# A fused attention and mixture-of-experts kernel: routing steps left in line, three batches counted, other slots for query scaling and scatters

## The chip, the cores and the metric

The kernel runs on one core of a Trainium2 chip. The metric is device time in microseconds for one execution. Its engines are TensorE (PE, whose weight loads the profile lists as PEld), VectorE (DVE), ScalarE (ACT), GpSimd (POOL) and SyncE (SP). Each works through its own queue in order, and they wait for each other on semaphores. SP issues plain DMAs here; POOL issues the indirect ones, which gather or scatter rows by a list of row numbers.

## The reference

```python
B, H, S, D = 8, 8, 576, 64            # attention, causal in blocks of 64
scores = q @ k.T / sqrt(D);  scores[block_i < block_j] = -1e9
attn = exp(scores - max) / (sum + 1e-9)
x = (attn @ v), heads side by side     # 4608 rows of 512
logits = x @ w_gate + modality_bias[modality_id]      # 8 experts
e = argmax(logits);  g = softmax(logits)[e]
out = g * (relu(x @ w1[e]) @ w2[e])    # 512 -> 1024 -> 512, one expert per row
```

With the inputs drawn here three experts get rows: 2289, 2153 and 166 of the 4608. After three batches the counts are 828, 736 and 164, after four 1114, 1026 and 164.

## The kernel before

**Attention** runs over 32 pairs of heads, four pairs to a batch. The table `ORDER` is written out by hand: it is one slot, in which the queues of all engines get the steps of pair p = slot (first half) and of pair slot − 1 (second half). `S0` to `S3` are score products (L202), `M` row maxima on DVE (L209), `E` exponentials on ACT (L222), `T` transposes on PE (L229), `C` copies of them out of PSUM (L234, units 0, 1 and 5 on DVE, the others on ACT), `V` the products with v (L248), `O` copies of their results, `D` the inverse of the sums, `B` products with the identity and the gate weights (L268), `Z0` and `Z1` the scaled rows (L287). `L` loads q and k of a pair two slots ahead through SP, and `Q` scales q of the next pair on POOL (L184). The score products of slot n + 1 need `Q` of slot n. Six PSUM banks are shared: `S0` of the next slot writes the bank that `C0` has to empty first, `S1` that of `C1`.

**Routing.** After `Z1` of the last pair of a batch (slots 4, 8, ..., 32), SP stores the batch's rows in DRAM (L294, eight DMAs), and `routing` returns 19 small steps, mostly on DVE: logits, a product on PE (`total`), bias, maximum, exponential on ACT, one-hot, weight, stores, counts on PE, running positions. The names `q1` to `q6`, `qp` and `qv` in `ORDER` are the places where the next of them is taken off the list. Steps that are left when the next batch's `Z1` comes are emitted there at once. The last step leaves five scatters in `placing`; each is a small DVE add (L394) and a POOL scatter of 128 rows of 64 bytes into a list of row numbers by expert (L395), taken at `S0` and at `T0`.

**Choosing.** After EARLY = 4 batches `choose` appends 22 DVE steps (kind "c", L99) that pick the expert with most rows (a) and the next one (b). From slot 21 on `EARLY_STEPS` then does part of the experts' work inside the slots: `stage` loads weights of expert a through SP (L641, L644), `prep` splits them on POOL in eight instructions (L584, L585), `ids` loads row numbers, and `fetch` gathers 128 rows (L667) from the batches that were counted.

**The experts** work in segments of 256 rows: four `up` products of 24 matmuls (L706), each followed by a relu on ACT (L712) and its low part on DVE (L713); transposes of the next segment's rows (L688); two `down` products of 24 matmuls (L752), each with an output scatter on POOL (L755). Three lead segments use rows of the counted batches. `LAST` is slot 32: the end of the last pair woven with the `up` of the first lead segment. `run_all` then does its two `down`, the rest of the last batch's routing, all scatters that are left (`flush`), the loads of the lists for the other segments (L662), and loops over the segments; n = 1 is the second lead segment.

Of the kernel before, what the change touches and what calls it, by code (L numbers as in the profile page):

```python
# [25 lines left out]
PPB = H // 2  # L26
# [7 lines left out]
NROW = NE * REGION  # L34
COVER = SLOT * NSLOT
COVER_B = COVER - FEW
EARLY, NLEAD = 4, 3
LEAD = SLOT * NLEAD
BIG = float(1 << 20)
NWARM = 12  # L40
# [26 lines left out]
PARTS = (("idf", (128,)), ("ii", (128,)), ("iom8", (NE,)), ("iom40", (5, NE)), ("iov40", (5, NE)), ("inv5", (5,)), ("first5", (NE, 5)), ("base8", (NE,)), ("edges", (N // SLOT,)))  # L67

ORDER = (
# [3 lines left out]
)  # L73

EARLY_STEPS = {
    (21, "S0"): ("stage", "stage"), (21, "T0"): ("prep",),
    **{(slot, "T0"): ("stage", "prep") for slot in range(22, 29)},
    (28, "S0"): ("ids",), (29, "S0"): ("stage",),
    (30, "S0"): ("fetch",), (30, "T0"): ("fetch",),
    (31, "S0"): ("fetch",), (31, "T0"): ("fetch",),  # L80
}
LAST = (
    ("+turn0", 0), ("V", 1), ("O", 1), ("D", 1), ("+up0", 0), ("+relu", 0), ("B", 1), ("Z0", 1), ("Z1", 1), ("+place", 0), ("+up1", 0), ("+relu", 0), ("+up2", 0), ("+steps3", 0), ("+up3", 0), ("+place", 0),
    ("+relu", 0), ("+relu", 0), ("+turn1", 0), ("+steps2", 0),
)


# [20 lines left out]
def attention_moe(ctx, tc, qk, vr, bkw, mid, mb, w1, w2, cf, ci, ld, out):  # L108
# [382 lines left out]
    def run_slot(slot):  # L491
        nonlocal steps, ex
        if slot < NPAIR - 1:
            load_v(slot + 1)
        for name, stage in LAST if slot == NPAIR else ORDER:
            p = slot - stage
            if placing and slot < NPAIR and name in ("S0", "T0"):
                g, c = placing.pop(0)
                g(c)
            for what in EARLY_STEPS.get((slot, name), ()):  # L500
                if ex is None:
                    ex = Experts(ctx, tc, cst, scratch, btmp, con["edges"], xrows, idlist, idf, w1, w2, out, sel, run, base8, pick, dot, banks, (o0, banks[5]), placing, staging, extra, xrb)
                ex.early(what)
            if name[0:6] == "+steps":
                for f in steps[0 : int(name[6:])]:
                    f()
                steps = steps[int(name[6:]) :]
                continue
            if name[0] == "+":
                ex.early(name[1:])  # L510
                continue
            if name[0] == "q":
                kind = "" if name[1].isdigit() else name
                kinds = (kind,) if kind else ("", "c")
                quick = bool(steps) and getattr(steps[0], "kind", "") == "c"
                for _ in range(1 if kind else 3 if quick else 1 + (slot == PPB * EARLY + 1)):
                    if slot > 1 and steps and getattr(steps[0], "kind", "") in kinds:
                        steps.pop(0)()
                continue
            if not 0 <= p < NPAIR:  # L520
                continue
            emit(name, p)
            if name == "Z1" and p % PPB == PPB - 1:
                for f in steps:
                    f()
                steps = routing(p // PPB)
                if p // PPB == EARLY - 1:
                    choose(Later(dve, steps))

# [15 lines left out]


class Experts:
    def __init__(self, ctx, tc, cst, scratch, btmp, edges, xrows, idlist, idf, w1, w2, out, sel, run, base8, pick, dot, banks, ys, placing, staging, extra, xrb):
        self.__dict__.update(locals())
        self.nc = tc.nc  # L550
        self.turn, self.hturn = 0, 0
        self.er, self.w = {}, {}
        self.staged = []
        self.todo = [(k, name, c) for name in "abc" for k in range(2) for c in range(4)]
        self.sturn, self.sbank, self.tbank = 0, 0, 0
        flat = xrb[0].rearrange("p s q d -> p (s q d)")
        self.xg = [flat[:, 2 * XW * i : 2 * XW * i + 2 * XW].rearrange("p (a w) -> p a w", a=2) for i in range(2)]

        def cut(i, a, n=1024):
            return extra[:, i : i + n].rearrange("p (a f) -> p a f", a=a)  # L560

        self.w["a", 1] = [[cut(1024 * (4 * x + c), 2) for c in range(4)] for x in range(2)]
        self.xth, self.xtl = cut(1024 * 8, 4), cut(1024 * 9, 4)
        self.hidden = [[cut(1024 * (10 + i) + 512 * x, 2, 512) for x in range(2)] for i in range(4)]
        self.w["a", 0] = [cut(1024 * 14 + SHIFT + 4096 * x, 4, 4096) for x in range(2)]
        self.parts = []
# [9 lines left out]
    def early(self, what):  # L576
        if what == "stage":
            self.stage()
        elif what == "prep":
            st, k, name, c = self.staged[0]  # L580
            flat = [t.rearrange("p a f -> p (a f)") if len(t.shape) > 2 else t for t in (st, *self.target(k, name, c))]
            for i in range(4):
                s, h, l = (t[:, 256 * i : 256 * i + 256] for t in flat)
                self.nc.gpsimd.tensor_copy(h, s)  # L584
                self.nc.gpsimd.tensor_tensor(l, s, h, ALU.subtract)  # L585
            self.staged.pop(0)
        elif what == "ids":
            ids = self.load_ids(self.sel["ra"], 0, LEAD, "lead", ET.SP)
            self.plan = [(ids, 2 * t, "a", EARLY * S) for t in range(NLEAD)]
        elif what == "fetch":  # L590
            if not self.parts or not self.parts[-1].left:
                self.parts.append(self.fetch(*self.plan[len(self.parts)], early=True))
            s = self.parts[-1]
            row = self.cst.tile([128, 1], I32, name="row", bufs=4)
            self.nc.vector.tensor_copy(row, s.ids[:, s.t + s.left[0] : s.t + s.left[0] + 1])
            self.gather(s, row)
        elif what[0:4] == "turn":
            self.turn_rows(self.parts[int(what[4])], True)
        elif what[0:2] == "up":
            self.up_products(self.parts[0], int(what[2]))  # L600
        elif what == "place":
            if self.placing:
                g, c = self.placing.pop(0)
                g(c)
        elif what == "relu":
            self.up_relu(self.parts[0])
        elif what == "flush":
            self.flush()
# [164 lines left out]
        dve.tensor_copy(counti, count)  # L773
        return counti

    def run_all(self, steps):
        tc, ctx, nc, cst, sel, plan = self.tc, self.ctx, self.nc, self.cst, self.sel, self.plan
        dve = nc.vector
        self.wk = wk = ctx.enter_context(tc.tile_pool(name="wk", bufs=1, side="right", reuse_waits="tile"))
        self.w["b", 0] = [wk.tile([128, 4, DF], F32R, name=f"w0{x}b") for x in "hl"]  # L780
        wk.tile([128, SHIFT], F32R, name="pad0")
        w2 = [wk.tile([128, 2, DM], F32R, name=f"w1b{i}") for i in range(8)]
        wk.tile([128, SHIFT], F32R, name="pad1")
        self.w["b", 1] = [w2[0:4], w2[4:8]]
        s, nxt = self.parts
        later = self.fetch(*plan[2])
        self.down(s, 0)
        for f in steps[0:9]:
            f()
        self.down(s, 1)  # L790
        for f in steps[9:]:
            f()
        self.flush()
        s, nxt = nxt, later
        self.rem, left = (cst.tile([128, NE], F32, name=n) for n in ("rem", "left"))
        self.rowc, self.expc = (cst.tile([128, 1], I32, name=n) for n in ("rowc", "expc"))
        idsa = self.load_ids(sel["rr"], 0, COVER - LEAD, "a")
# [3 lines left out]
        idsc = self.load_ids(self.rowc, 0, SLOT, "c", most=NROW - SLOT)  # L801
        dve.tensor_tensor(left, self.run, sel["start"], ALU.subtract)
        self.more = self.trips(left)

        plan += [(idsa, 2 * t, "a") for t in range(NSLOT - NLEAD)]
        plan += [(idsb, 2 * t, "b") for t in range(NSLOT - 1)]
        plan += [(idsb, 2 * NSLOT - 2, "b", N, 1), (idsc, 0, "a")]
        for n in range(1, len(plan)):
            if s.parts == 1:
                self.up_few(s)  # L810
            else:
                for m2 in range(4):
                    self.up(s, m2)
                    if m2 == 1 and n < NSLOT:
                        self.convert(True)
            later = None
            if s.parts == 1:
                self.turn_few(s, 0)
# [1 line left out]
                self.hturn += 2  # L820
            if nxt is not None:
                self.turn_rows(nxt)
                if n + 2 < len(plan):
                    later = self.fetch(*plan[n + 2])
            if n >= NSLOT and self.staged:
                self.convert()
# [83 lines left out]
```

## Time and profile before

| | |
|---|---|
| three runs | 747.29, 748.56, 749.25 us; median 748.56 |
| the profiled execution | 747.08 us |
| its span, first to last instruction | 745.4 us |
| mean granted TensorE clock | 0.989 |
| PE busy | 724.3 us (97%) |
| DVE, ACT, POOL busy | 345.0, 332.2, 242.6 us |

Times in rows count from the first instruction of the profiled execution. A row of a timeline gives the start, the time until the last of the merged instructions ends, engine, line, operation, what it writes and reads, how many, and in brackets the idle time before it with what ended it. Attention fills about the first 300 us, the segments the rest.

### The profile page before, as it was taken

The numbers are of one execution on the slowest core, as the hardware profiler recorded it, in microseconds if no ns is written. First come the engines' busy times: TensorE is split into PE (matmuls) and PEld (weight loads), VectorE is DVE, ScalarE is ACT, GpSimd is POOL, SyncE is SP. The second block draws the span as 40 slices with busy tenths as digits, with TensorE's granted clock in tenths as the row PEclk, the third lists the DMA queues.
The fourth block names the chain that finished last, engine by engine and source line by source line (L and its number), as shares of the span: only waits on it lengthen the run. The fifth ranks groups of instructions, "written<-read, shape, count | busy, mean of one in ns | idle before, by whom it ended". The sixth has DMA issues, their size and how long they took to land. (4 is left out here: it accounts for less than half of the span.)

```text
span 745.4 us, 19432 instructions
## 1 busy us (share of the span) xinstructions
PE 724.3 (97%) x7800; PEld 633.5 (85%) x7800; DVE 345.0 (46%) x1036; ACT 332.2 (45%) x974; POOL 242.6 (33%) x326
## 2 busy tenths in 40 slices
PE   8999999999989999989999999999999999999995
PEld 5888888888778888978999889998899988999794
DVE  4888888988989987421221112211222122221220
ACT  5888877888767876212222222221222222221220
POOL 2223343433399964155223132232111221112101
PEclk9999999999999999998999999999999999999998
DMA  5476456464667672313221222213121221201000
GB/s 183 127 213 215 125 165 168 138 177 137 156 194 238 197 209 78 90 34 73 78 79 36 79 72 86 72 43 100 50 79 48 81 86 45 84 30 47 29 15 20
DMA packets 41916, 77.80 MB, mean 104 GB/s; under 512 B 12170, under 2 KB 24266, under 8 KB 41824
## 3 DMA queue, kind: packets, MB, share of 16 engines
q1 hardware_dynamic: 34336, 57.02, 26.3%
q0 software_dynamic: 7488, 19.52, 8.4%
q8 instruction: 62, 1.02, 0.6%
q14 instruction: 30, 0.25, 0.1%
HBM read 54.86 MB, written 22.25 MB: 103 GB/s over the span
## 5 line engine op out<-in xcount | busy, mean ns | idle before, releaser
L713 DVE SCALAR_TENSOR_TENSOR extra<-bank,extra 128x512 fp32r<-128x512 f32 x72 | 49.8, 692 | 313.8 <-ACT extra L712 313.8
L222 ACT ACTIVATE pm<-bank,nm 128x512 f32<-128x512 f32 (+3 forms) x320 | 155.6, 500 | 64.9 <-DVE nm L209 60.0
L209 DVE TENSOR_REDUCE nm<-bank 128x1 f32<-128x512 f32 (+3 forms) x320 | 121.0, 447 | 6.5 <-PE bank L202 6.0
L706 PE MATMUL bank<-extra 128*128 128x256 f32 x960 | 119.4, 285 | 2.7 <-issue 2.7
L706 PEld LDWEIGHTS bank<-extra 128*128 128x128 f32 x960 | 117.7, 192 | 4.4 <-issue 3.6
L712 ACT ACTIVATE extra<-bank 128x512 fp32r<-128x512 f32 x72 | 43.1, 598 | 158.6 <-PE bank L706 149.1
L229 PE MATMUL bank<-cf,pm 128*128 128x128 f32 (+1 forms) x736 | 90.7, 279 | 3.3 <-ACT pm L222 3.3
L706 PE MATMUL bank<-extra,w0hb 128*128 128x256 f32 x512 | 91.1, 280 | 0.0
L202 PE MATMUL bank<-raw,q 64*64 64x512 f32 (+7 forms) x1280 | 87.8, 407 | 2.5 <-POOL q L184 2.5
L229 PEld LDWEIGHTS bank<-cf,pm 128*128 128x128 f32 (+1 forms) x736 | 79.5, 140 | 11.3 <-ACT pm L222 7.0
L184 POOL TENSOR_SCALAR q<-raw 128x144 f32<-128x144 f32 x124 | 67.7, 573 | 59.4 <-PE bank L229 47.9
L202 PEld LDWEIGHTS bank<-raw,q 64*64 64x64 f32 x1280 | 54.9, 134 | 30.2 <-issue 21.1
L706 PEld LDWEIGHTS bank<-extra,w0hb 128*128 128x128 f32 x512 | 79.0, 188 | 0.7
L248 PE MATMUL b<-pt,v 64*64 64x64 f32 (+3 forms) x896 | 77.0, 267 | 0.9 <-issue 0.6
L248 PE MATMUL o<-pt,v 64*64 64x64 f32 (+3 forms) x896 | 72.5, 262 | 1.0 <-issue 1.0
L706 PE MATMUL bank<-extra,w0lb 128*128 128x256 f32 x256 | 71.8, 280 | 0.0
L755 POOL DMA_INDIRECT out<-scratch,ids_b x17 | 16.9, 994 | 161.8 <-ACT scratch L754 161.8
L234 DVE COPY pt<-bank 128x512 f32<-128x512 f32 (+1 forms) x96 | 59.2, 642 | 21.2 <-PE bank L229 15.6
L222 ACT ACTIVATION_READ_ACCUMULATOR pm<-bank,nm 128x1 f32 x320 | 65.2, 204 | 0.0
L395 POOL DMA_INDIRECT idlist<-idt,pi x40 | 40.3, 1008 | 73.8 <-DVE pi L394 67.6
L248 PEld LDWEIGHTS b<-pt,v 128*64 128x64 f32 (+1 forms) x896 | 54.7, 136 | 3.9 <-issue 1.0
L752 PE MATMUL o<-extra 128*128 128x512 f32 x240 | 57.2, 394 | 0.0
(149 smaller groups left out, 992.0 us busy)
## 6 DMA issues: line engine op xcount, KB each, us to landing
raw<-qk SPq DMA_DIRECT2D x31, 576.0 KB
v<-vr SPq DMA_DIRECT2D x32, 384.0 KB
staging<-w SPq DMA_DIRECT2D x24, 256.0 KB
staging<-w SPq DMA_DIRECT2D x12, 512.0 KB
xrows<-xr SPq DMA_DIRECT2D x16, 256.0 KB
xrows<-xr SPq DMA_DIRECT2D x32, 128.0 KB
idlist<-btmp SPq DMA_DIRECT2D x8, 304.0 KB
xrows<-xr SPq DMA_DIRECT2D x16, 64.0 KB
```

The lines of the kernel that those rows point to most:

```text
L184: pool.tensor_scalar(d.q[:, i : i + 144], d.raw[:, i : i + 144], SCALE, None, ALU.mult)
L202: pe.matmul(place(s, a, b)[64 * t : 64 * t + 64], d.q[hs, D * s : D * s + D], d.k[hs, a:b], start=True, stop=True)
L209: dve.tensor_reduce(d.nm[:, i : i + 1], place(s, a, b), AX.X, ALU.max, negate=True)
L222: act.activation(d.pm[:, o : o + b - a], place(s, a, b), AF.Exp, bias=d.nm[:, s : s + 1], scale=1.0, accum_out=total)
L229: pe.transpose(banks[g][0:m, 128 * i : 128 * i + 128], d.pm[:, o : o + m], idf)
L234: dve.tensor_copy(dst, src) if g in ON_DVE else act.copy(dst, src)
L248: pe.matmul(o.rearrange("p (n c) -> p n c", c=64), d.v[rows, h, block, :], x, start=start, stop=stop)
L395: last = pool.indirect_dma_start(idlist[:], bass.IndirectOffsetOnAxis(ap=g.pi[c], axis=0), g.idt[:, c, :], None, bounds_check=NROW - 1, oo ...
L706: nc.tensor.matmul(hp[:, a, :], w[:, kc, ms], x[:, kc, :], start=i == 0, stop=i == len(mm) - 1)
L712: self.nc.scalar.activation(hh, hp, AF.Relu)
L713: self.nc.vector.scalar_tensor_tensor(hl, hp, 0.0, hh, ALU.max, ALU.subtract)
L752: nc.tensor.matmul(y, s.hs[m][x][:, ts], self.part(w, 1, m // 2)[:, m % 2, :], start=n == 0, stop=n == len(mm) - 1)
```

## The change

Nothing of the arithmetic changes. `EARLY` is 3, so choosing and the lead segments use three batches, and choosing begins four slots earlier. `Q` moves from behind `O` to behind `S1`. The scatters are taken at `V` and `T3` instead of `S0` and `T0`. Steps that are left at a batch's `Z1` stay at the head of the list; up to three steps are taken at a place from slot 29 on, two while more than 20 are left. The first two `stage` go from slot 21 to slot 20, one from slot 29 to 30. In slot 30 the gathers are at `S0` and `T0` as before, in slot 31 one remains, and three are in `LAST`. The last batch's routing runs wholly inside `LAST`; scatters are taken one at a time in `LAST`, ahead of each `down` of the first segment and after each `up` of the second; the list loads follow as `lists()`.

```diff
-EARLY, NLEAD = 4, 3
+EARLY, NLEAD = 3, 3
+HURRIED = 29
 ORDER = (
-    ("S0", 0), ("S1", 0), ("M0", 0), ("qv", 1), ("E0", 0), ...
-    ("L", -2), ("V", 1), ("q1", 1), ("E4", 0), ("O", 1), ("Q", -1), ("q2", 1), ("q3", 1), ("q4", 1),
+    ("S0", 0), ("S1", 0), ("Q", -1), ("M0", 0), ("qv", 1), ("E0", 0), ...
+    ("L", -2), ("V", 1), ("q1", 1), ("E4", 0), ("O", 1), ("q2", 1), ("q3", 1), ("q4", 1),
 EARLY_STEPS = {
-    (21, "S0"): ("stage", "stage"), (21, "T0"): ("prep",),
+    (20, "S0"): ("chosen", "stage", "stage"), (21, "T0"): ("prep",),
     **{(slot, "T0"): ("stage", "prep") for slot in range(22, 29)},
-    (28, "S0"): ("ids",), (29, "S0"): ("stage",),
-    (30, "S0"): ("fetch",), (30, "T0"): ("fetch",),
-    (31, "S0"): ("fetch",), (31, "T0"): ("fetch",),
+    (28, "S0"): ("ids",), (30, "S0"): ("fetch", "stage"), (30, "T0"): ("fetch",),
+    (31, "T0"): ("fetch",),
 LAST = (
-    ("+turn0", 0), ("V", 1), ("O", 1), ("D", 1), ("+up0", 0), ("+relu", 0), ("B", 1), ("Z0", 1), ("Z1", 1), ("+place", 0), ("+up1", 0), ("+relu", 0), ("+up2", 0), ("+steps3", 0), ("+up3", 0), ("+place", 0),
-    ("+relu", 0), ("+relu", 0), ("+turn1", 0), ("+steps2", 0),
+    ("+turn0", 0), ("V", 1), ("O", 1), ("D", 1), ("+up0", 0), ("+relu", 0), ("+fetch", 0), ("B", 1), ("Z0", 1), ("Z1", 1), ("+steps1", 0), ("+up1", 0), ("+relu", 0),
+    ("+place", 0), ("+steps13", 0), ("+up2", 0), ("+relu", 0), ("+place", 0), ("+steps5", 0), ("+up3", 0), ("+place", 0), ("+relu", 0), ("+turn1", 0), ("+fetch", 0), ("+fetch", 0),
 # run_slot
-            if placing and slot < NPAIR and name in ("S0", "T0"):
+            if placing and slot < NPAIR and name in ("V", "T3"):
-                for _ in range(1 if kind else 3 if quick else 1 + (slot == PPB * EARLY + 1)):
+                for _ in range(1 if kind else 3 if quick else 3 if slot >= HURRIED else 1 + (len(steps) > 20)):
             if name == "Z1" and p % PPB == PPB - 1:
-                for f in steps:
-                    f()
-                steps = routing(p // PPB)
+                steps = steps + routing(p // PPB)
 # Experts.run_all
-        later = self.fetch(*plan[2])
-        self.down(s, 0)
-        for f in steps[0:9]:
-            f()
-        self.down(s, 1)
-        for f in steps[9:]:
-            f()
-        self.flush()
+        s, nxt, later = self.parts
+        for i in range(2):
+            self.early("place")
+            self.down(s, i)
...
                     self.up(s, m2)
                     if m2 == 1 and n < NSLOT:
                         self.convert(True)
+                    if n == 1:
+                        self.early("place")
+            if n == 1:
+                self.lists()
```

## Rows read from the trace of the kernel before

**Rows 1.** The page's busy times: us, share of the span, instructions.

```profile
PE 724.3 (97%) x7800; PEld 633.5 (85%) x7800; DVE 345.0 (46%) x1036; ACT 332.2 (45%) x974; POOL 242.6 (33%) x326
```

**Rows 2.** Timeline of PE: first score products of slots, 16 to 30; last, LAST.

```profile
145.62 0.59 PE L202 MATMUL bank<-raw,q 64*64 64x512 f32 x2
154.17 0.59 PE L202 MATMUL bank<-raw,q 64*64 64x512 f32 x2
163.10 0.60 PE L202 MATMUL bank<-raw,q 64*64 64x512 f32 x2
...
200.02 0.60 PE L202 MATMUL bank<-raw,q 64*64 64x512 f32 x2
...
211.69 2.70 PE L202 MATMUL bank<-raw,q 64*64 64x512 f32 x40 [2.51 <-POOL q L184]
...
273.19 0.61 PE L202 MATMUL bank<-raw,q 64*64 64x512 f32 x1
...
293.88 0.33 PE L688 MATMUL bank<-cf,xr 128*128 128x128 f32 x1
```

**Rows 3.** Timelines of PE, POOL and SP, 189 to 212 us: slots 21 and 22.

```profile
189.26 0.59 PE L202 MATMUL bank<-raw,q 64*64 64x512 f32 x2
...
203.56 0.39 POOL L584 CAST extra<-staging 128x256 fp32r<-128x256 f32 x1 [5.15 <-DMA staging<-w]
...
209.45 2.19 POOL L184 TENSOR_SCALAR q<-raw 128x144 f32<-128x144 f32 x4
...
198.24 2.60 SPq L641 DMA_DIRECT2D staging<-w  x4
```

**Rows 4.** Timeline of DVE: maxima of slot 17, then choosing at slots 20 and 21.

```profile
155.56 3.95 DVE L209 TENSOR_REDUCE nm<-bank 128x1 f32<-128x512 f32 x10
...
190.84 0.22 DVE L99 SCALAR_TENSOR_TENSOR kx<-cnb,mx_b,cf 128x8 f32<-128x8 f32 x1
...
192.74 3.73 DVE L209 TENSOR_REDUCE nm<-bank 128x1 f32<-128x512 f32 x10
```

**Rows 5.** Timelines, 324 to 364 us: products of the second and third segments, ACT, POOL.

```profile
322.41 7.58 PE L706 MATMUL bank<-extra 128*128 128x256 f32 x62
...
340.08 1.04 PE L688 MATMUL bank<-cf,xr 128*128 128x128 f32 x8
...
351.89 11.52 PE L706 MATMUL bank<-extra 128*128 128x256 f32 x96
363.25 1.04 PE L688 MATMUL bank<-cf,xr 128*128 128x128 f32 x8
...
336.46 0.60 ACT L712 ACTIVATE extra<-bank 128x512 fp32r<-128x512 f32 x1 [9.51 <-remote]
...
324.79 0.97 POOL L395 DMA_INDIRECT idlist<-idt,pi  x1 [0.30 <-DVE kx_c L413]
...
333.72 0.97 POOL L395 DMA_INDIRECT idlist<-idt,pi  x1 [0.30 <-issue]
```

**Rows 6.** Windows: each engine's busy time, then granted clock, DMA share and GB/s.

```profile
330.00:340.00 10.00, 7.33 (x34) 6.73 (x35) 1.38 (x2) 2.03 (x3) 7.66 (x8) 0.66 0.09 5
...
510.00:520.00 10.00, 10.00 (x71) 9.30 (x70) 0.69 (x1) 1.44 (x3) 3.84 (x4) 1.00 0.29 86
```

**Rows 7.** Timeline of POOL, 515 to 519 us: an output scatter and two gathers.

```profile
515.23 0.99 POOL L755 DMA_INDIRECT out<-scratch,ids_a  x1 [4.44 <-ACT scratch L754]
...
517.86 1.02 POOL L667 DMA_INDIRECT xr<-xrows,ids_b  x1 [0.30 <-issue]
```

**Rows 8.** Timelines of POOL and PE in slot 31: last of three indirect DMAs.

```profile
286.14 1.01 POOL L667 DMA_INDIRECT xr<-xrows,row  x1 [0.31 <-issue]
...
287.73 0.25 PE L248 MATMUL o<-pt,v 64*64 64x64 f32 x1 [0.40 <-issue]
```

**Rows 9.** Timelines of DVE and ACT in slot 18: first copies, routing's exponential.

```profile
169.40 1.28 DVE L234 COPY pt<-bank 128x512 f32<-128x512 f32 x2
...
171.19 0.28 ACT L336 ACTIVATE ex<-df 128x40 f32<-128x40 f32 x1
```

More of the change, by code (lines that the diff above doesn't have):

```diff
@@ L501, in run_slot @@
                 if ex is None:
-                    ex = Experts(ctx, tc, cst, scratch, btmp, con["edges"], xrows, idlist, idf, w1, w2, out, sel, run, base8, pick, dot, banks, (o0, banks[5]), placing, staging, extra, xrb)
+                    ex = Experts(ctx, tc, cst, scratch, btmp, con["edges"], xrows, idlist, idf, w1, w2, out, sel, run, base8, pick, dot, banks, (o0, banks[5]), placing, staging, extra, xrb, lambda kind: any(getattr(f, "kind", "") == kind for f in steps))
                 ex.early(what)
@@ L547, with __init__ @@
 class Experts:
-    def __init__(self, ctx, tc, cst, scratch, btmp, edges, xrows, idlist, idf, w1, w2, out, sel, run, base8, pick, dot, banks, ys, placing, staging, extra, xrb):
+    def __init__(self, ctx, tc, cst, scratch, btmp, edges, xrows, idlist, idf, w1, w2, out, sel, run, base8, pick, dot, banks, ys, placing, staging, extra, xrb, steps_left):
         self.__dict__.update(locals())
@@ L578, in early @@
             self.stage()
+        elif what == "chosen":
+            assert not self.steps_left("c")
         elif what == "prep":
@@ L774, in trips, with lists @@
         return counti
[L776 to L785, printed above, removed]
-        later = self.fetch(*plan[2])
-        self.down(s, 0)
-        for f in steps[0:9]:
-            f()
-        self.down(s, 1)
-        for f in steps[9:]:
-            f()
+    def lists(self):
+        cst, sel, dve = self.cst, self.sel, self.nc.vector
         self.flush()
-        s, nxt = nxt, later
         self.rem, left = (cst.tile([128, NE], F32, name=n) for n in ("rem", "left"))
@@ L803, in run_all @@
         self.more = self.trips(left)
[L805 to L808, printed above, removed]
+        self.plan += [(idsa, 2 * t, "a") for t in range(NSLOT - NLEAD)]
+        self.plan += [(idsb, 2 * t, "b") for t in range(NSLOT - 1)]
+        self.plan += [(idsb, 2 * NSLOT - 2, "b", N, 1), (idsc, 0, "a")]
+    def run_all(self, steps):
+        tc, ctx, plan = self.tc, self.ctx, self.plan
+        self.wk = wk = ctx.enter_context(tc.tile_pool(name="wk", bufs=1, side="right", reuse_waits="tile"))
+        self.w["b", 0] = [wk.tile([128, 4, DF], F32R, name=f"w0{x}b") for x in "hl"]
+        wk.tile([128, SHIFT], F32R, name="pad0")
+        w2 = [wk.tile([128, 2, DM], F32R, name=f"w1b{i}") for i in range(8)]
+        wk.tile([128, SHIFT], F32R, name="pad1")
+        self.w["b", 1] = [w2[0:4], w2[4:8]]
+        assert not steps
+        s, nxt, later = self.parts
+        for i in range(2):
+            self.early("place")
+            self.down(s, i)
+        s, nxt = nxt, later
+        count = 2 * NSLOT + 1
+        for n in range(1, count):
             if s.parts == 1:
@@ L822, in run_all @@
                 self.turn_rows(nxt)
-                if n + 2 < len(plan):
+                if n + 2 < count:
                     later = self.fetch(*plan[n + 2])
```

2 rows, old and new, of the table ORDER are left out of this document.

## The prediction

> **What bounds the kernel.** I read the page's busy times first: TensorE is busy for 97% of the span [rows 1], so no other engine's saving counts by itself. A change that moves small work can win only where TensorE stands still or is stretched. I therefore read the list of waits and then TensorE's timeline for every gap and for the starts of the slots. An ordinary slot with routing in it, slot 17, takes 163.10 − 154.17 = 8.93 us [rows 2]; I use it as the norm. Four places are longer.
>
> Slot 21 takes 200.02 − 189.26 = 10.76 us, slot 22 takes 11.67 us [rows 2, 3]. Slots 30 and 31 together, up to the first transpose of `LAST`, take 293.88 − 273.19 = 20.69 us [rows 2], where two norms are 17.86. The `up` products of the second segment (n = 1) take 340.08 − 322.41 = 17.67 us, those of the third 363.25 − 351.89 = 11.36 us [rows 5]. The excesses are 1.83, 2.74, 2.83 and 6.31 us: 13.7 us is all that there is to win on this reading.
>
> **What each excess is.** In slot 21 VectorE's maxima start 192.74 − 189.26 = 3.48 us into the slot, in slot 17 at 155.56 − 154.17 = 1.39 us [rows 2 to 4]. Between stand 13 choosing steps that the leftover loop emits after `Z1`, from 190.84 to the maxima: 1.9 us, so some 0.14 us a step [rows 4]. The exponentials and then the transposes come later by that.
>
> In slot 22 the score products of slot 23 wait 2.51 us for the scaled queries [rows 2]. POOL scales from 209.45, because `prep` began only at 203.56, when its weights landed, which SP had issued at 198.24 behind the batch's row stores [rows 3].
>
> In the second segment no semaphore explains the stretch. POOL issues eight scatters from 324.79 to 333.72, one every 1.28 us [rows 5]. ScalarE waits 9.51 us for the second `up`, to 336.46 [rows 5], though its 48 matmuls lie within the first 62, listed from 322.41 without a pause. TensorE's granted clock is 0.66 in the window from 330 [rows 6]: part of it at the lower level, after TensorE had stopped and started. The end comes when the train of scatters ends. Slots 30 and 31 show the same in small: in slot 31 a scatter and two gathers stand in a row, the last from 286.14, and TensorE is idle by "issue" before 287.73 [rows 8].
>
> A rule of the Trainium skill speaks against this reading: SBUF — State Buffer, section "SBUF: two separate sides", says that engine ports and DMA ports cannot contend and that TensorE never waits on anyone there. By that rule the scatters would be bystanders of the stall, and spreading them would leave it. The rows show the stall only inside trains, and the rule says nothing of semaphores or issue, so I go by the rows.
>
> **The change part by part.**
>
> *Scatters of the last batches.* Of the nine left, three lie in `LAST`, two ahead of the `down` of the first segment, four behind the `up` of the second, one per 24 matmuls, that is per 11.36/4 = 2.84 us [rows 5], so each (about 1 us) is followed by a pause. The nearest row for what remains is a train of three at 515.23 to 518.88, in a window in which TensorE is busy 10.00 of 10 us at clock 1.00 [rows 6, 7]. So I take the whole excess: −6.3 us; the other bound is 1 us for each of the four scatters, −2.3 us. The list loads now follow the fourth `up`. Behind them on POOL are the gathers for the fourth segment and the two output scatters; the gathers are needed one `down` pair and four `up` later, over 20 us, so they are covered. If that cover were gone, each microsecond late would be one on TensorE.
>
> *Query scaling first.* 2.2 us of POOL work [rows 3] now stands ahead of `prep`. What is late next is `prep` itself (with the scatter behind it 5.9 us, from 203.56 to 209.45 [rows 3]), for which nothing on TensorE waits before the segments. A scatter at `T3` can now lie behind `prep` and ahead of the next `Q`; even 4 us into the slot, `Q` ends at 6.2 of 8.9. Its other wait is the load of q and k, which SP issues behind the row stores; that wait exists today. The earlier `stage` also gets ahead of those stores. I take the gap: −2.5 us (bounds −2.74 and 0).
>
> *Leftover steps in line, three batches.* All 22 steps stay: 13 in slot 16, 9 in slot 17, three at a place, most of them ahead of `C0`. 22 × 0.14 = 3.1 us. In slot 20 today 9 of them (1.3 us) run unseen, before the flush. Slot 16 should hide as much, slot 17 about 0.5 us of VectorE's waiting. That leaves 1.3 against 1.83: −0.5 us (bounds −1.8 and +1.3, all 3.1 in the open). With three batches expert a has 828 rows, over the 768 of the lead segments, and the experts chosen are the same: no segment more or fewer.
>
> *Slots 30 and 31.* One gather each replaces trains of two and three, and a stage load no longer stands ahead of the last q and k: the 2.83 us should go. But the hurried routing puts bias to weight into one slot. `weight` on VectorE waits for the exponential on ScalarE, which stands behind `O`: in slot 18 it ends 171.19 + 0.28 − 163.10 = 8.37 us into the slot, where `C0` starts at 169.40 − 163.10 = 6.30 [rows 2, 9]. Queued behind `weight` are `C0`, `C1`, `D`, the rows and the next maxima. With `weight`, guard and reciprocal (three dependent steps, some 0.2 us each) `C0` starts at about 9.05, its bank is free at 9.7, and `S0` of slot 31, due at 8.9, is 0.8 us late. The maxima follow some 1.1 us late on top. So +1.9, and −0.9 net (bounds −2.8, no cost, and +1.0, if the remaining gathers also stretch the products as today).
>
> *Scatters at `V` and `T3`.* 31 scatters lie in the slots, 12 of them move from the head of a slot to behind its maxima. Slot 16, with one scatter at `T0`, takes 154.17 − 145.62 = 8.55 us, slot 17, with a second one at `S0` and the `total` product on TensorE, 8.93 [rows 2]: so a scatter costs between 0 and 0.38 us. Those from the head no longer delay the maxima, those at `T3` may delay signals to the last copy and the rows. I take 0, the two against each other; bounds −4.6 us (12 × 0.38 saved) and +11.8 (31 × 0.38 added).
>
> *`LAST` and `down`.* Routing steps move from VectorE's idle time in `down` to idle time between `up`; counts on TensorE may wait for the one-hot: ten steps at 0.14 plus a relu of 0.6 us and about as much for its low part are 2.6 us against an `up` of 2.84 [rows 4, 5]. I take +0.1 (bounds 0 and 1).
>
> Sum: −6.3 − 2.5 − 0.5 − 0.9 + 0.1 = **−10.1 us**. The profiled execution took 747.08, so it would be 737.0; the median of the three runs shown is 748.56, 1.5 above, so the forecast for a median is **738.5 us**.
>
> **The rivals.**
>
> *The train is a bystander* (the rule above): the second segment stays at 17.67 and only 3.8 us go: 744.8. Against it: the stall ends with the train [rows 5]. 0.08.
>
> *The hurried steps and the choosing cost their upper bounds*: +1.9 in slots 30 and 31 and +1.8 at slot 16 above my terms, part of it hidden: about 741.5. For it: VectorE is the engine that paces ScalarE, and the steps are dependent. 0.17.
>
> *Neither costs anything*: 2.8 + 1.8 instead of 1.4: 735.3. 0.10.
>
> *The new places hurt (the other side).* A scatter at `T3` falls on the signals of the last transposes, of `B` and of the next `S0`; each would hold `C5`, rows and maxima. With 31 scatters it takes 10.1/31 = 0.33 us each to eat the gain, and 0.4 us for over 0.3% slower: at 0.5 us each 754. Against it: 0.38 us is the whole difference between slots 16 and 17, and the `total` product has its share in it. 0.04.
>
> *`Q` gains nothing*, because the load of q and k is what it waits for: 741.0. It lies in the range, with 0.05 out of the forecast's share.
>
> **How the numbers follow.** Forecast 0.56, then 0.17, 0.10, 0.08, 0.05, 0.04. The likeliest time is 738.5, its own range 736.5 to 740.5. Reaching to the dear and the cheap case it is 735 to 743.5, which leaves out the bystander and the slow case, 0.12, and a little of the tails. 0.3% is 2.2 us, about what a measurement of this kernel can tell from no change. Below 746.3 lies everything but the last rival and part of the bystander's tail: faster 0.93, same 0.03, slower 0.04.
>
> **What would show it.** Right: the `up` of the second segment in 11.4 to 12 us, ScalarE's long wait and the lower clock gone there; no wait for `q` on PE near slot 22; slots 20 to 22 near 8.9, slots 16 to 18 longer by some 1.3 together; in slot 30 a VectorE wait for `ex`. Wrong: the stretch persists with spread scatters; `S0` waits for `q` or for a bank in every slot; the slots with scatters at `V` and `T3` all grow.

## The result, and the profile after

The changed kernel takes 742.06 us (median of 4 runs, 741.80 to 742.83), the kernel before 748.57 beside it: ratio 0.9916 with a 95% interval of 0.9904 to 0.9928. It is faster, by 6.5 us where 10.1 were forecast; the time lies in the range, 3.6 us above the predicted one and outside the likeliest case's own range. The profiled execution took 741.80 us with a span of 740.1, 5.3 less than before; the profiled execution of the kernel before (747.08) is shorter than all four timed ones (747.29 to 749.25), so the two traces account for 5.3 us and not for all of the 6.5.

TensorE's busy time hardly moved, as the page's first line shows against [rows 1]: the gain is idle or stretched time.

```profile
PE 723.7 (98%) x7800; PEld 630.2 (85%) x7800; DVE 345.7 (47%) x1038; ACT 332.4 (45%) x974; POOL 243.5 (33%) x326
```

The timeline of TensorE in the changed kernel: the first score products of slots 9, 10, 17, 18, 19, 21, 22, 23, 30 and 31, then the transposes of the first two segments and the `up` of the second. It answers to [rows 2, 3, 5].

```profile
83.45 0.60 PE L202 MATMUL bank<-raw,q 64*64 64x512 f32 x2
...
92.69 0.59 PE L202 MATMUL bank<-raw,q 64*64 64x512 f32 x2
...
156.19 0.59 PE L202 MATMUL bank<-raw,q 64*64 64x512 f32 x2
...
166.03 0.60 PE L202 MATMUL bank<-raw,q 64*64 64x512 f32 x2
...
175.98 0.59 PE L202 MATMUL bank<-raw,q 64*64 64x512 f32 x2
...
193.61 0.59 PE L202 MATMUL bank<-raw,q 64*64 64x512 f32 x2
...
202.90 0.59 PE L202 MATMUL bank<-raw,q 64*64 64x512 f32 x2
...
211.72 0.59 PE L202 MATMUL bank<-raw,q 64*64 64x512 f32 x2
...
272.56 0.60 PE L202 MATMUL bank<-raw,q 64*64 64x512 f32 x2
...
282.99 1.15 PE L202 MATMUL bank<-raw,q 64*64 64x512 f32 x6 [0.55 <-POOL wt L373]
...
292.98 0.60 PE L688 MATMUL bank<-cf,xr 128*128 128x128 f32 x4 [0.38 <-issue]
...
311.74 0.60 PE L688 MATMUL bank<-cf,xr 128*128 128x128 f32 x4
...
323.32 11.52 PE L706 MATMUL bank<-extra 128*128 128x256 f32 x96
334.68 1.04 PE L688 MATMUL bank<-cf,xr 128*128 128x128 f32 x8
```

The `up` of the second segment are one unbroken row of 334.68 − 323.32 = 11.36 us, where they took 17.67 [rows 5], at full clock, as the window shows that answers to [rows 6]:

```profile
330.00:340.00 10.00, 10.00 (x69) 9.23 (x69) 5.45 (x25) 2.90 (x5) 6.40 (x5) 1.00 0.22 56
```

Slots 21 and 22 now take 9.29 and 8.82 us, and the wait for scaled queries is gone. But slot 17 grew from 8.93 to 9.84 us, slot 18 to 9.95, slot 9 to 9.24, and `LAST` (292.98 to 311.74) from 16.65 to 18.76. In the kernel before `LAST` runs from 293.88 [rows 2] to the transposes of the second segment:

```profile
310.53 1.03 PE L688 MATMUL bank<-cf,xr 128*128 128x128 f32 x8
```

VectorE's timeline says why in five rows. At the head of slots 11 and 18 the scaled rows (L287) wait for `B`; the profile names the products that stand next to those of `B` in TensorE's queue. In slot 17 the maxima start 158.75 − 156.19 = 2.56 us into the slot, against 1.39 in the kernel before [rows 2, 4]: six of the choosing steps of slot 16 run ahead of them at the head of slot 17. `weight` in slot 30 waits for ScalarE, and the rows of pair 30, in the last batch, wait 2.21 us.

```profile
102.90 0.49 DVE L287 TENSOR_TENSOR xr<-o,inv 128x320 f32<-128x320 f32 x1 [0.98 <-PE bank L202]
...
158.75 3.72 DVE L209 TENSOR_REDUCE nm<-bank 128x1 f32<-128x512 f32 x10
...
167.54 0.49 DVE L287 TENSOR_TENSOR xr<-o,inv 128x320 f32<-128x320 f32 x1 [1.21 <-PE bank L202]
...
281.64 0.20 DVE L357 TENSOR_REDUCE sm<-ex 128x5 f32<-128x40 f32 x1 [0.98 <-ACT ot L256]
...
294.70 0.49 DVE L287 TENSOR_TENSOR xr<-o,inv 128x320 f32<-128x320 f32 x1 [2.21 <-PE bank L688]
```

Ahead of the last one stand three indirect transfers in a row on POOL, a gather and two scatters:

```profile
290.24 1.03 POOL L667 DMA_INDIRECT xr<-xrows,row  x1 [4.60 <-DVE pi L394]
291.58 1.00 POOL L395 DMA_INDIRECT idlist<-idt,pi  x1 [0.30 <-DVE pt L234]
292.88 0.98 POOL L395 DMA_INDIRECT idlist<-idt,pi  x1 [0.30 <-issue]
```

The third is the first scatter written in `run_all`; it was issued ahead of the place where the kernel's text has it (the experiment that moves it takes it out of this row).

This table has the stretches that changed, all from such timelines, in us: a slot from its first score product to the next one's, `LAST` and the second segment from first transpose to first transpose. The kernels of the columns are explained with the experiments. The first four columns are of chip 1. "Chip 1" stands for the chips of the first two sets of measurements, in which the kernel before takes 748.57 and 747.92 us, "chip 2" for three other chips, on which it takes 739.31, 739.19 and 739.27; that there are two kinds came out only in the second set of experiments. All measurements near 748 were taken before all near 739, so that a difference of chips is not told apart here from something that changed in between. The start up to slot 2 is left out, and so are stretches that stayed: the start varies by 1.2 us (22.2 to 23.4) between kernels that are alike there.

| stretch | before | after | old places | one moved | before, chip 2 | after, chip 2 | last version, chip 2 |
|---|---|---|---|---|---|---|---|
| slots 9 to 11 | 26.53 | 27.45 | 26.52 | 27.34 | 26.35 | 26.27 | 26.35 |
| 13 to 15 | 26.56 | 28.18 | 27.77 | 28.18 | 26.35 | 27.52 | 26.35 |
| 17 to 19 | 26.53 | 28.87 | 27.34 | 28.84 | 26.35 | 27.44 | 26.99 |
| 21 to 23 | 31.03 | 26.83 | 27.03 | 26.78 | 33.20 | 26.28 | 26.58 |
| 25 and 26 | 18.31 | 17.56 | 18.18 | 17.57 | 18.19 | 17.55 | 17.66 |
| 30 and 31 | 20.69 | 20.42 | 20.35 | 19.87 | 18.08 | 19.49 | 18.42 |
| LAST | 16.65 | 18.76 | 18.62 | 17.85 | 16.65 | 17.21 | 17.21 |
| second segment | 29.55 | 22.94 | 22.92 | 22.94 | 23.32 | 22.92 | 22.91 |

The differences of the second and the first column add up to −4.8 of the 5.3 us; the other 0.5 is the start. The two traces of the kernel before differ by 8.3 us: 6.2 in the second segment, 2.6 in slots 30 and 31, 0.7 in the other slots of the table and 0.9 in the start, less 2.2 that slots 21 to 23 take more on chip 2.

### The profile page after: what moved, and what is told of

It is laid out like the page before. It is cut to its first block, busy times and chain, and to the rows that moved or that the text cites. A ratio compares the mean times of both kernels' runs of the same rounds, so it can differ in the third digit from the quotient of the medians.

```text
span 740.1 us, 19430 instructions
## 1 busy us (share of the span) xinstructions
PE 723.7 (98%) x7800; PEld 630.2 (85%) x7800; DVE 345.7 (47%) x1038; ACT 332.4 (45%) x974; POOL 243.5 (33%) x326
## 2 busy tenths in 40 slices
DMA packets 41916, 77.80 MB, mean 105 GB/s; under 512 B 12170, under 2 KB 24266, under 8 KB 41824
## 5 line engine op out<-in xcount | busy, mean ns | idle before, releaser
L706 PE MATMUL bank<-extra 128*128 128x256 f32 x960 | 116.0, 281 | 0.0
L706 PEld LDWEIGHTS bank<-extra 128*128 128x128 f32 x960 | 115.1, 188 | 1.0 <-issue 0.2
L202 PE MATMUL bank<-raw,q 64*64 64x512 f32 (+7 forms) x1280 | 90.1, 407 | 0.8 <-POOL wt L373 0.6
L202 PEld LDWEIGHTS bank<-raw,q 64*64 64x64 f32 x1280 | 56.9, 134 | 29.1 <-issue 20.7
```

Source lines behind the costliest of these rows:

```text
L202: pe.matmul(place(s, a, b)[64 * t : 64 * t + 64], d.q[hs, D * s : D * s + D], d.k[hs, a:b], start=True, stop=True)
L706: nc.tensor.matmul(hp[:, a, :], w[:, kc, ms], x[:, kc, :], start=i == 0, stop=i == len(mm) - 1)
```

## The experiments

**The train put back.** Eight scatters in a row again, behind the first segment's `down`:

```diff
-("+up2", 0), ("+relu", 0), ("+place", 0), ("+steps5", 0), ("+up3", 0), ("+place", 0)
+("+up2", 0), ("+relu", 0), ("+steps5", 0), ("+up3", 0)
     for i in range(2):
-        self.early("place")
         self.down(s, i)
+    self.flush()
...
-                    if n == 1:
-                        self.early("place")
```

> The changed kernel, but its eight last scatters again stand in one train on POOL, directly behind the down products of the first segment (n = 1's activations), where the kernel before had its train; everything else of the change stays. Train theory (scatters of GpSimd in a row hold up TensorE): the up products of the second segment take about 17 us again instead of 11.4, with a lower granted clock in them, and from its first to its second turn about 29 us instead of 22.9; LAST, freed of three scatters, gives back 0 to 2 us; together 746 to 748 us, +4 to +6 against the changed kernel. Bystander theory (the train does not matter, something else of the change shortened the segment): the up products stay at 11.4 us and the time is 740 to 742.

Measured: 743.03 us, ratio 0.9936 (0.9911 to 0.9961), span 743.1. The timelines of TensorE, ScalarE and POOL:

```profile
322.38 10.66 PE L706 MATMUL bank<-extra 128*128 128x256 f32 x88
333.48 0.73 PE L706 MATMUL bank<-extra 128*128 128x256 f32 x4 [0.44 <-issue]
334.91 0.63 PE L706 MATMUL bank<-extra 128*128 128x256 f32 x4 [0.70 <-issue]
335.63 0.33 PE L688 MATMUL bank<-cf,xr 128*128 128x128 f32 x1
...
336.40 1.09 ACT L712 ACTIVATE extra<-bank 128x512 fp32r<-128x512 f32 x2 [6.36 <-PE bank L706]
...
324.86 0.98 POOL L395 DMA_INDIRECT idlist<-idt,pi  x1 [0.31 <-issue]
...
333.81 0.97 POOL L395 DMA_INDIRECT idlist<-idt,pi  x1 [0.30 <-issue]
```

The picture of [rows 5] is back, smaller: TensorE runs 88 of the 96 products, then four at a time with stops by issue, ScalarE gets no finished `up` for 6.36 us and gets it when the train ends. The `up` take 335.63 − 322.38 = 13.25 us, not 17; the clock is 0.66 from 336 to 341, and the next segment is 2.2 us longer. Together that is 4.0 of the 6.6 us, less 1.2 that slots 30, 31 and `LAST` give back, 2.8 of the 3.0 us by which the span is longer.

```profile
336.00:341.00 5.00, 4.67 (x18) 4.04 (x19) 3.62 (x17) 2.15 (x4) 3.52 (x3) 0.66 0.50 80
```

The timed runs show less, 1 to 1.5 us, with a wide interval, where the train theory had 4 to 6; 743.03 lies between the two theories. The profiled execution is the slowest of the four (744.71 us, mean clock 0.993; the others 742.76 to 743.29 at 0.997), so the trace shows the stall at its largest. On this chip the stall comes back with the train, but not at its old size; what sets the size wasn't tried.

**The scaling put back behind `O`.**

```diff
-("S0", 0), ("S1", 0), ("Q", -1), ("M0", 0)
+("S0", 0), ("S1", 0), ("M0", 0)
-("O", 1), ("q2", 1)
+("O", 1), ("Q", -1), ("q2", 1)
```

> The changed kernel with one thing undone: the scaling of the queries stands behind O again, so on POOL behind the weight preparation; the earlier stage loads stay. Theory that the place of the scaling was the cause: slots 21 and 22 grow by about 2.5 us together, as a wait of TensorE for the scaled queries of about that size; about 744.5 us, +2.5. Rival, that the earlier loads alone cured it: no such wait, 742.0 within 0.5.

Measured: 742.77 us, ratio 0.9940 (0.9924 to 0.9956), chip 1. TensorE's wait for `q` behind slot 22 is 0.41 us, not 2.5:

```profile
210.89 1.08 PE L202 MATMUL bank<-raw,q 64*64 64x512 f32 x8 [0.41 <-POOL q L184]
```

The earlier load had cured slot 22 without the new order (9.31 us, where it was 11.67 and is 8.82 with both); the order itself is worth 0.7 us of span, the net of small waits over all slots.

**The first load put back to slot 21**, the scaling left first (chip 2):

```diff
-(20, "S0"): ("chosen", "stage", "stage"), (21, "T0"): ("prep",)
+(20, "S0"): ("chosen",), (21, "S0"): ("stage", "stage"), (21, "T0"): ("prep",)
```

> The changed kernel with one thing undone: the first two weight tiles are loaded at the head of slot 21 again, behind the row stores on SP, as in the kernel before; the scaling of the queries stays first in the slot. With the experiment that put the scaling back it fills the square of the two edits (scaling first or not, load early or not), of which both together took 2.85 us from slot 22, and the early load alone 2.36. Theory that either of them cures the wait alone, as the prediction had it for the scaling: slot 22 stays at 8.8 to 9.2 us, total within 0.5 us. Rival, that the load is the cause: preparation starts some 3.5 us into slot 22 and takes 4.4, the scaling for slot 24 or the one of its own slot stands behind it on GpSimd, and slots 22 and 23 grow by 1 us or more together.

Measured: 741.66 us, slower than the kernel before on the same chip, ratio 1.0034 (1.0020 to 1.0049), and 6.4 above the changed kernel on a chip of that kind. POOL, then SP, then TensorE's wait:

```profile
204.08 0.39 POOL L584 CAST extra<-staging 128x256 fp32r<-128x256 f32 x1 [7.20 <-DMA staging<-w]
...
209.94 2.20 POOL L184 TENSOR_SCALAR q<-raw 128x144 f32<-128x144 f32 x4
...
198.76 2.59 SPq L641 DMA_DIRECT2D staging<-w  x4
...
212.19 1.12 PE L202 MATMUL bank<-raw,q 64*64 64x512 f32 x4 [4.10 <-POOL q L184]
```

The weights are issued on SP behind the row stores again, land late, `prep` waits for them at the head of POOL, and the scaling, though first in its slot, stands behind that `prep`. With both experiments the square is full, though one corner lies on chip 1 and this one on chip 2: the load is the cause. The new order by itself cures nothing; on chip 2 the kernel before, with late load and old order, waits 2.99 us there, and the new order 4.10.

**The slots' scatters at `S0` and `T0` again.**

```diff
-if placing and slot < NPAIR and name in ("V", "T3"):
+if placing and slot < NPAIR and name in ("S0", "T0"):
```

> The changed kernel with one thing undone: the scatters of the slots stand at S0 and T0 again instead of V and T3. Theory that a scatter at T3 holds the transposes of B and with them the rows and maxima (0.3 to 0.8 us in each of slots 9, 11, 13 to 15, 17 and 18): 1 to 3 us less, 739 to 741 us, and the rows of slots 9 and 11 start about 0.4 us into the slot instead of 1.0 to 1.25. Theory of the prediction (the two places cost the same, 0): 742 within 0.7. Theory that the new places save what a scatter cost at the head of a slot: 743 to 746.

Measured: 740.12 us, ratio 0.9902 (0.9876 to 0.9927), chip 1: 1.9 us below the changed kernel, with intervals that overlap; the slots decide. Column "old places": slots 9 to 11 lose all of their growth, 17 to 19 1.5 of 2.3 us, 13 to 15 0.4 of 1.6; slots 25 and 26 grow by 0.6 again. VectorE's timeline of slot 9, in the changed kernel and then in this one:

```profile
84.46 0.49 DVE L287 TENSOR_TENSOR xr<-o,inv 128x320 f32<-128x320 f32 x1 [0.84 <-PE o L268]
```

```profile
83.09 0.49 DVE L287 TENSOR_TENSOR xr<-o,inv 128x320 f32<-128x320 f32 x1 [0.21 <-PE o L268]
```

The changed kernel's scatter at `T3` starts at 82.92 and ends at 84.01; the products of `B` under it are seen late. `V` and `T3` were put back together, so their shares aren't told apart.

**One scatter moved in `LAST`**, so that only two indirect transfers stand in a row:

```diff
-("+turn1", 0), ("+fetch", 0)
+("+turn1", 0), ("+place", 0), ("+fetch", 0)
     for i in range(2):
-        self.early("place")
+        if i:
+            self.early("place")
```

> The changed kernel with one scatter moved: the first one after the first segment's turn in run_all now stands behind that turn in the written order of LAST, so that it is no third in a row behind the gather and the scatter before it. Theory that the row of three at 290 to 294 us is what holds the rows of the last batch and so lengthens LAST by 2.1 us: LAST falls from 18.8 to about 17 us and the time to 740 to 740.7. Rival, that the other scatters of LAST lengthen it one by one: LAST stays at 18.8 and the time at 742 within 0.5.

Measured: 740.36 us, ratio 0.9908 (0.9880 to 0.9936). `LAST` is 17.85, the rows of the last batch wait 0.86 instead of 2.21, and slot 31 gains 0.46: of the 2.1 us that `LAST` had lost, 0.9 were the third transfer, half of what the theory had for it.

**Work added to the sixth segment**: eight scatters, eight copies, eight plain transfers (the changed kernel's results stay as they are).

```diff
     self.up(s, m2)
+    if n == 5 and m2 == 0:
+        self.extra_load(8)
```

> The changed kernel with work added: eight scatters of GpSimd (128 rows of 64 bytes each, into tables that nobody reads), one right behind the other, after the first up of the sixth segment (n = 5), where the changed kernel has none and its four up take 11.4 us with TensorE never idle. Train theory: those up are stretched, to between 13.3 us (as in the experiment with the train put back) and 17.7 (as in the kernel before), with idle time of TensorE by issue, ScalarE waiting over 5 us for a finished up until the train ends, and a lower granted clock after it; 2 to 6 us more in all. Bystander theory: the four up stay at 11.4 us and the clock at 1.00, the time rises by less than 0.5 us.

> The changed kernel with work added at the place of the train of eight scatters: eight plain copies on GpSimd, 128x640 fp32 each, about as long as a scatter, in one row. It asks whether it is a busy GpSimd as such (its port into SBUF, its load) that holds TensorE. Theory that the indirect transfers hold it: nothing, the four up of n = 5 stay at 11.4 us, total within 0.5 us. Theory that any work of GpSimd without a pause does: the up stretch to 13 us or more.

> The changed kernel with work added at the same place: eight plain transfers of the same size (128 rows of 64 bytes each) on SP's queue. It asks whether it is small packets on the DMA rings as such that hold TensorE. Theory that it is GpSimd's indirect issue: nothing, 11.4 us for the four up of n = 5, total within 0.5 us. Theory that many small packets do: 13 us or more.

Measured: 736.00, 735.25 and 734.58 us, one run each, beside 739.31 for the kernel before: another kind of chip. The train of eight, and TensorE under it:

```profile
412.06 0.97 POOL L781 DMA_INDIRECT spare<-xr,ids_lead  x1 [0.30 <-issue]
...
420.98 0.97 POOL L781 DMA_INDIRECT spare<-xr,ids_lead  x1 [0.30 <-issue]
...
409.54 11.52 PE L707 MATMUL bank<-extra 128*128 128x256 f32 x96
420.90 1.04 PE L689 MATMUL bank<-cf,xr 128*128 128x128 f32 x8
```

Nothing is held: 11.36 us, as the bystander theory had it, and the same with the copies and the plain transfers. What the train adds, about 0.5 us, lies behind the last transposes of the kernel. None of the three says anything about chip 1.

**The same once more, with the kernel before.**

> The same kernel as in the first look with eight added scatters in a row, once more, since that look was on a chip on which the kernel before takes 739.3 us and not 748, and on which the scatters at T3 cost nothing either. If this chip is like the first (the kernel before near 748): train theory, the four up of n = 5 take 13.3 to 17.7 us with TensorE idle by issue and ScalarE waiting over 5 us; theory that a train alone holds nothing and that it needs what stands around it in the second segment: 11.4 us here too. If it is like the second chip: 11.4 us under both.

> The kernel before itself, profiled on the chip that this call gets, beside the kernel with the added train. Theory that the hold in a train of scatters is a property of the chip: where the kernel before takes about 739, its second segment's up are 11.4 to 12 us with a clock near 1.00 and the train of eight in them all the same, and the slot 22 wait of about 2.5 us for the scaled queries is still there; where it takes about 748, they are 17.7 us as before. Rival, that something else of that chip is faster: the up stay near 17 us at 739 and all slots are shorter.

Measured: 736.63 and 738.76 us, again on chip 2 (739.19). The train in the sixth segment holds nothing here either. The decisive rows are those of the kernel before on this chip, its eight scatters and its second segment:

```profile
322.79 0.97 POOL L395 DMA_INDIRECT idlist<-idt,pi  x1 [0.30 <-DVE kx_c L413]
...
331.74 0.97 POOL L395 DMA_INDIRECT idlist<-idt,pi  x1 [0.30 <-issue]
...
320.40 11.61 PE L706 MATMUL bank<-extra 128*128 128x256 f32 x96
331.85 1.04 PE L688 MATMUL bank<-cf,xr 128*128 128x128 f32 x8
...
326.42 0.60 ACT L712 ACTIVATE extra<-bank 128x512 fp32r<-128x512 f32 x1 [2.24 <-PE bank L706]
```

The same instructions at the same spacing of 1.28 us, and the `up` take 11.45 us instead of 17.67. The hold isn't in the kernel alone: it needs a train and something that differed between chip 1 and chip 2.

**The changed kernel on chip 2, and a version with what was learnt.** The version takes the old places of the slots' scatters, the moved scatter of `LAST`, and:

```diff
-("q1", 1), ("E4", 0), ("O", 1), ("q2", 1)
+("q1", 1), ("E4", 0), ("q2", 1), ("O", 1)
-shifted, hits, expo, hit_index
+shifted, expo, hits, hit_index
-for _ in range(1 if kind else 3 if quick else 3 if slot >= HURRIED else 1 + (len(steps) > 20)):
+for _ in range(1 if kind else (3 if name in ("q5", "q6") else 1) if quick else 3 if slot >= HURRIED else 1):
```

> The changed kernel itself, on the chip that this call gets, beside the version below. If this chip holds TensorE in a train of scatters, as the first did (the kernel before near 748): ratio 0.9916 again, slot 9 at 9.2 us and LAST at 18.8. If it does not (the kernel before near 739): theory that the change then lives on slots 21 to 23 and 25 to 26 (7.6 us less) and pays for the hurried and doubled routing (slots 14, 15, 17, 30, 31 and LAST, 4.3 us more), 0.4 less in the second segment: about -4 us, 735, ratio 0.994 to 0.996, slot 9 at 8.7 and LAST at 17.2. Rival, that the spread scatters were the whole gain: 1.000 there.

> The changed kernel with what the runs spoke for: the scatters of the slots at S0 and T0 again, the first scatter of run_all behind the turn of LAST, the exponential ahead of the hits in the routing and the step before O, no two steps at a time, and choosing steps three at a time only behind C0 and C1 (one at a time ahead of them). Theory that the wait of weight for ScalarE inside one slot, the choosing steps ahead of C0 and (where a train holds) the scatters' places are what the change lost: 1.3 us in slots 14 and 15, 0.5 to 0.9 in 17, up to 1 in 30 and 31, and 2 to 3 more on a chip of the first kind; 732 to 733 on the second kind, 736.5 to 738 on the first. Rival, that VectorE's work only moves and is paid elsewhere: as the changed kernel within 0.7 us on the second kind.

Measured: the changed kernel 735.27 us (734.52 to 735.73), ratio 0.9947 (0.9929 to 0.9964); the version 733.37 (732.56 to 733.90), ratio 0.9923 (0.9905 to 0.9940). On chip 2 the change gains on slots 21 to 23 and 25 to 26 (7.6 us) and loses in 13 to 19 (2.3), 30 and 31 (1.4) and `LAST`. Its wait in slot 14, on VectorE:

```profile
135.52 0.20 DVE L357 TENSOR_REDUCE sm<-ex 128x5 f32<-128x40 f32 x1 [1.40 <-ACT ex L336]
```

The same step of slot 30 waits in the changed kernel on chip 2 and, the second row, waits for nothing in the version:

```profile
277.48 0.20 DVE L357 TENSOR_REDUCE sm<-ex 128x5 f32<-128x40 f32 x1 [1.15 <-ACT ex L336]
...
274.58 0.19 DVE L357 TENSOR_REDUCE sm<-ex 128x5 f32<-128x40 f32 x1
```

Slots 13 to 15 lose all of their 1.17 us, 30 and 31 1.07 of 1.41, 17 to 20 only 0.27 net: there the choosing steps are paid elsewhere, as the rival said. The version beats both kernels on chip 2, a little above the forecast 732 to 733; on chip 1 it wasn't run.

## Why the prediction was right, and where not

The time lies in the range in part by luck. It fell near the 741.5 of the rival *the hurried steps and the choosing cost their upper bounds*, but not for that rival's reason: those steps cost less than their bounds, and what was missing from the sum was `LAST` (2.0 us) and the places of the scatters (2.3 us).

*Scatters of the last batches*, −6.3: the second segment gained 6.61. For chip 1 the size was right, and the train put back brought the stall back, at 4.0 of the 6.6 us. On chip 2 this term is 0.4 us, and it is not the train: two small products and one of `down` moved into `LAST`. The rule of the Trainium skill, SBUF — State Buffer, section "SBUF: two separate sides", by which I had read these scatters as bystanders, agrees with chip 2 (11.45 us under the train) and fails as a forecast on chip 1 (17.67); what the rows show held there is TensorE's issue and its finished signals, of which the section says nothing. I had 0.08 for the bystander; I had no case in which the kernel before has a stall on one chip and none on another.

*Query scaling first*, −2.5: slot 22 lost 2.85 us: the size came out, but by another way, and the step that gave the gap to the new order failed. The load a slot earlier, which the prediction had in one sentence and without a price, took 2.36 of it alone; without it the new order leaves a wait of 4.1 us. The mistake was that `prep` is work "for which nothing on TensorE waits before the segments": the next scaling stands behind it on POOL, and TensorE waits for that.

*Leftover steps in line, three batches*, −0.5: slot 21 gave 1.47 as hoped. Slots 13 to 19 grew by 4.0, of which 1.9 go with the places of the scatters (old places). So choosing and doubled routing cost 2.0 against 1.5: about +0.5, and +0.2 with the old places, where slot 21 gives 1.8; on chip 2 it is +0.2, too. Missed was slot 14: counting the waiting steps makes two go at a time, and `weight` meets its exponential in one slot, the very wait that I had worked out for slot 30.

*Slots 30 and 31*, −0.9: −0.27. The wait for ScalarE stood where it was forecast (0.98 us, `S0` of slot 31 0.55 late). On chip 2, where no train of the kernel before had to be paid back, the term is +1.4: the cost of +1.9 was 0.5 too dear, and the saving existed on chip 1 only.

*Scatters at `V` and `T3`*, 0: this is the term that failed: the two effects do not cancel. By the old places it is about +2.3 us on chip 1, and the rival "the new places hurt" named its mechanism, a scatter over `B`; its sign, that all slots with such scatters grow, came in part (9, 11, 13 to 15 and 17 to 19 grew, 25 and 26 fell); at 2.3/31 = 0.07 us each the price was a fifth of the 0.33 that would have eaten the gain. On chip 2 slots 9 to 11 didn't change and 25 and 26 gained 0.6.

*`LAST` and `down`*, +0.1: +2.1. I had read the scatters' places in the kernel's text; the order of issue put the first one of `run_all` earlier and made three in a row. One moved gives 0.9 back, and 0.46 in slot 31. Another 0.56 came with two products of the last batch and one of `down` that now lie in `LAST` and no more in the second segment, which is 0.4 shorter for it (chip 2). The last 0.6 is there on chip 1 only; which of the other scatters it belongs to wasn't tried.

Left open: what makes trains of indirect transfers hold TensorE on chip 1. Copies and plain transfers were only tried on chip 2, where the train itself holds nothing, so they don't tell it. It is not a fetch of instructions under way: from 324 to 340 us the trace of the kernel before has packets of GpSimd's queue alone. One rival that wasn't tried is the recording itself. The timed runs have a recorded span and clock, too, and for the same 41916 DMA packets of the kernel before the trace holds 4514 semaphore updates by DMAs on chip 1 and 5097 on chip 2 (4448 to 4531 in all traces of chip 1, 5064 to 5200 in those of chip 2). The two kinds differ in what was recorded, too.

## What to carry to other kernels

Follow a wait to the head of the in-order queue: here the remedy was the late load that a preparation waited for, and not the place of the work stuck behind it. Where several small dependent steps go into one slot, check the step that waits for another engine first. Time a change that lives on a stall on more than one chip: the same edit was worth 0.84% on one kind and 0.53% on the other, and in other places.

## What the runs showed of the hardware

Chips ran the same program at 748 us in the first two sets of measurements and at 739 in the later three, each steadily (ten runs of 746.03 to 749.23 on one; thirteen of 737.11 to 741.08 on another). The instructions and the spacing of the eight scatters were the same; only in the first did TensorE stop by issue and ScalarE wait 9.5 us, to 336.46, for products that the trace has done by 330 [rows 5].

TensorE's clock was at its lower level, 1.2 GHz, for part of a stretch after a stop on either kind: the window's mean is 0.66 from 336 to 341 with the train put back, and on chip 2 0.66 around its 2.99 us wait for `q` in the kernel before, where slot 23 then took 10.28 us instead of the 8.73 of the changed kernel. After the 2.51 us wait at the same place on chip 1 [rows 2] it stayed at full speed, the third row:

```profile
210.74 3.92 PE L202 MATMUL bank<-raw,q 64*64 64x512 f32 x26 [2.99 <-POOL q L184]
...
210.00:215.00 5.00, 4.26 (x48) 2.70 (x50) 1.91 (x4) 1.95 (x7) 4.57 (x9) 0.66 0.51 129
...
212.00:217.00 5.00, 5.00 (x96) 3.91 (x88) 4.12 (x14) 3.46 (x13) 4.66 (x9) 1.00 0.56 173
```
